# Storing the two float32r parts of each word of w_in side by side in an attention + MLP kernel

## The chip, the cores and the metric

The kernel runs on one core of a Trainium2 chip. The time is device microseconds of one execution of the whole program. Beside the bare times there is one execution with the hardware profiler on; all rows of a profile come from it.

## The reference

Two stages. Attention over 8 batches x 8 heads, with 1152 keys of 64 values per head and the queries averaged in neighbouring pairs, so 576 queries per head. Its output, 4608 tokens x 512, is the input x of a two-matrix MLP with 2048 hidden units. All inputs and the output are float32.

```python
q_pool = q.reshape(B, H, S // 2, 2, D).mean(axis=3)
scores = (1 / sqrt(D)) * q_pool @ k.T
attn = exp(scores - max(scores)); attn = attn / (sum(attn) + 1e-9)
x = (attn @ v) as [B * S // 2, H * D]          # 4608 x 512
h = x @ w_in                                   # w_in 512 x 2048
g = h - tanh(h)
out = g @ w_out                                # w_out 2048 x 512
```

## The kernel before

**Two parts for each number.** [...] The arriving w_in and w_out are int64 words on the host's side, that is, two 32-bit words for each weight, and the kernel makes the high and the low float32r part of each weight itself.

**Preparing the weights (class `W`, lines 411 to 475).** It runs during attention, in 16 blocks: four of w_in (one for each 128 rows, columns 0 to 1023), four of w_out, four of w_in (columns 1024 to 2047), four of w_out. A block is 128 partitions x 1024 weights. `load` fetches the block twice, once as it is (`w_raw`) and once shifted by two bytes (`w_off`); both are seen as int32 with two words for each weight, and the views `self.hw` and `self.mid` take every second word. `steps` lists six steps, which attention takes from a list at fixed places, four for each head pair from the third pair on: `begin` (ScalarE, absolute value of w_raw into w_t), `clamp` (three VectorE instructions on w_t), `mid` (VectorE, w_off into the low half of the tile `w_hl`), `high` (VectorE, w_raw and w_t into the high half of w_hl; then the next block's loads are issued), an unnamed one (VectorE, high half of w_hl into w_t), and `low` (VectorE, low half of w_hl in place; then `store`). The tile w_hl exists once, so a block's `mid` waits until the stores of the block before have read it. In w_hl the 1024 high parts lie ahead of the 1024 low ones.

**Where the weights rest.** `store` writes w_hl to a scratch tensor in HBM: `wi_dram`, indexed by block f of 128 hidden units, partition, part s (high or low), row block c and hidden unit n; and `wo_dram` for w_out. For w_in it issues two DMAs on SyncE's queue, one for each part, each with runs of 128 words. Later `load_w` (line 101) fetches 128 x 1024 words for each of the 16 values of f, 4 KB in each partition, into whatever tile is free (w_raw, w_off, w_hl, w_t, raw, q, and tiles of their own named w), and keeps a view of it indexed by s, c and n in `wi[f]`.

**Attention.** 32 head pairs, each with 18 places of scores and exponentials and 18 places of P times V. Scores are four pairs of 64-row matmuls for each place; row maxima of the next pair are taken by VectorE from PSUM (mx). All PSUM results of this stage go through a ring of four buffers (ps). Into the last three pairs the first three steps of the MLP are put.

**The MLP.** 9 chunks of 512 tokens x 16 blocks of 128 hidden units = 144 steps. For each step `hidden` (line 165) issues twelve matmuls into ps_h: the weights are `wi[f][:, w, c]`, 128 x 128, and the moving operand is 512 tokens of x's high or low part (the very last step is done in two halves of 256 tokens). `shrink` then computes g on ScalarE, VectorE and GpSimd, and `second` issues twelve matmuls for the output two steps later; there g is the weight operand (g_hi, g_lo) and w_out moves.

**Order.** The order of each engine's instructions is as they are written out: `InOrder` (line 27) chains every instruction to the one before it on its engine, SyncE's DMA issues among them. The line numbers of most rows are therefore L37, the helper's; rows are told apart by tiles.

Of the kernel before, what the change touches and what calls it, by code (L numbers as in the profile page):

```python
# [7 lines left out]
F32 = mybir.dt.float32  # L8
F32R = mybir.dt.float32r
I32 = mybir.dt.int32  # L10
# [36 lines left out]
def attention_ffn_kernel(  # L47
# [16 lines left out]
    P = 128  # L64
    B, NP, _, _, SQ = q.shape
# [7 lines left out]
    DM, DFF = w_in.shape  # L73
    w_in, w_out = w_in.bitcast(U16), w_out.bitcast(U16)
    NF = DFF // P
    n_pair = B * NP
    pe, act, dve, pool, sp = (InOrder(tc, e) for e in (nc.tensor, nc.scalar, nc.vector, nc.gpsimd, nc.sync))

    const = ctx.enter_context(tc.tile_pool(name="const", bufs=1))
    dram = ctx.enter_context(tc.tile_pool(name="scratch", bufs=1, space=DRAM))  # L80
# [5 lines left out]
    s_dram = dram.tile([B, NP, 2, SQ], F32, name="s_dram")  # L86
    r_dram = dram.tile([B, NP, 2, SQ], F32, name="r_dram")
    m_dram = dram.tile([2, 2, P * 4 * 32], F32, name="m_dram")
    wi_dram = dram.tile([NF, P, 2, NP, P], F32, name="wi_dram")
    wo_dram = dram.tile([NF, P, 2, DM], F32, name="wo_dram")  # L90

    xp = [ctx.enter_context(tc.tile_pool(name="xp0", bufs=1))]
# [2 lines left out]
    wp = ctx.enter_context(tc.tile_pool(name="wp", bufs=1))  # L95
# [3 lines left out]
    wi, wo = {}, {}  # L99

    def load_w(tile_, f, which):

        t = tile_[:, which * 1024:(which + 1) * 1024] if tile_.shape[1] == 2048 else tile_[:, 0:1024]
        sp.dma_start(t.bitcast(F32), (wi_dram, wo_dram)[which][f].rearrange("p s n -> p (s n)" if which else "p s c n -> p (s c n)"))
        if which == 0:
            wi[f] = t.rearrange("p (s c n) -> p s c n", s=2, c=NP)
        else:
            wo[f] = t.rearrange("p (s n) -> p s n", s=2)

# [104 lines left out]
    def store(c, j):  # L214
        o = outp[0].tile([P, DM], F32, name="o_f")
        act.activation(o, c.po[j], AF.Copy)
        sp.dma_start(out[c.t0 + j * P:c.t0 + (j + 1) * P], o)
# [11 lines left out]
    with ExitStack() as actx:  # L229
# [178 lines left out]
        WN = 1024  # L408
        lo_b, hi_b = 2.0 ** -15, float.fromhex("0x1.dffffep+16")

        class W:
# [17 lines left out]
            def steps(self, then):  # L429
                ts, stt = dve.tensor_scalar, dve.scalar_tensor_tensor  # L430

                def f(x):
                    return x.bitcast(F32)

                def begin():
                    self.t = wp.tile([P, WN], I32, name="w_t")
                    act.activation(f(self.t), f(self.raw)[:, :, 1], AF.Abs)

                def mid():
                    self.hl = wp.tile([P, 2, WN], I32, name="w_hl")  # L440
                    ts(self.hl[:, 1], self.mid, 0x01FFFFFF, None, op0=ALU.bitwise_and)

                def clamp():
                    ts(f(self.t), f(self.t), lo_b, hi_b, op0=ALU.max, op1=ALU.min)
                    ts(self.t, self.t, 0x08000000, 3, op0=ALU.bitwise_xor, op1=ALU.logical_shift_left)
                    ts(self.t, self.t, 0x7FFFFFFF, None, op0=ALU.bitwise_and)

                def high():
                    stt(self.hl[:, 0], self.hw, -0x80000000, self.t, op0=ALU.bitwise_and, op1=ALU.bitwise_or)
                    if then:  # L450
                        then.load()

                def low():
                    stt(self.hl[:, 1].bitcast(F32R), self.hl[:, 1], 2.0 ** -36, f(self.t), op0=ALU.mult, op1=ALU.mult)
                    self.store()

                return [
                    begin,
                    clamp,
                    mid,  # L460
                    high,
                    lambda: ts(self.t, self.hl[:, 0], -0x800000, None, op0=ALU.bitwise_and),
                    low,
                ]

            def store(self):
                for s in range(2):
                    src = self.hl[:, s].bitcast(F32)
                    if self.kind == 0:
                        f0 = self.c // P  # L470
                        sp.dma_start(wi_dram[f0:f0 + WN // P, :, s, self.i].rearrange("f p n -> p f n"),
                                     src.rearrange("p (f n) -> p f n", n=P))
                    else:
                        sp.dma_start(wo_dram[self.i:self.i + 2, :, s].rearrange("f p n -> p f n"),
                                     src.rearrange("p (f n) -> p f n", n=DM))

        blocks = [W(0, r, 0) for r in range(NP)] + [W(1, i, 0) for i in range(0, 8, 2)]
        blocks += [W(0, r, WN) for r in range(NP)] + [W(1, i, 0) for i in range(8, 16, 2)]
# [45 lines left out]
        def first_weights(f, name, which):  # L524
            t = (wp if name[0] == "w" else rawp if name == "raw" else qp).tile(
                [P, {"w_t": 1024, "raw": KQ, "q2": 2 * SQ}.get(name, 2048)], F32R, name=name)
            for i in which:
                load_w(t, f, i)
# [28 lines left out]
        for pi in range(n_pair):  # L557
# [7 lines left out]
            n = pi + EARLY - n_pair  # L565
            if n == 0:
                c = Chunk(0)
# [29 lines left out]
    for f in range(NF):  # L597
        for which, have in enumerate((wi, wo)):
            if f not in have:
                load_w(wt.tile([P, 1024], F32R, name=f"w{which}_{f}"), f, which)  # L600
        if f == 7:
            nxt.fetch()
            for c in range(2):
                nxt.fetch_r(c)

    xs = None
    for ci in range(len(chunks)):
        if ci:
            c = Chunk(ci)
# [4 lines left out]
        for f in range(NF):  # L614
            n = ci * NF + f
            s = steps[n]
# [15 lines left out]
            if f == 1 and ci:  # L632
                for j in range(4):
                    store(steps[n - 2].chunk, j)
# [13 lines left out]
    for i, k in enumerate(b.parts):  # L648
        g_high(b, k)
        g_low(b, k)  # L650
        for j in range(2 * i, 2 * i + 2):
            second(b, [j])
            store(b.chunk, j)
# [38 lines left out]
```

## Time and profile before

| | us |
|---|---|
| median of 3 runs | 1580.03 |
| lowest and highest | 1577.24, 1580.16 |
| the profiled execution | 1580.02 |
| its span, from first to last instruction | 1578.3 |
| busy in it: TensorE matmul / weight load | 1556.5 / 1224.1 |
| busy in it: VectorE / ScalarE / GpSimd | 1185.8 / 978.3 / 1155.3 |

The granted TensorE clock is 0.999 over the span. PE is TensorE's matmuls, PEld its weight loads, which overlap the matmuls; DVE is VectorE, ACT ScalarE, POOL GpSimd, SP SyncE. A row of a group reads: line, engine, operation, output tile <- input tiles, partitions x elements, xcount | busy us, mean ns of one | idle us of the engine before them, and what ended it. Matmuls overlap each other and their ends are modelled, so the spacing of their starts says more than their lengths.

### The profile page before, as it was taken

Reading aid. Unit: us, or ns where it says so; the run is one execution under the profiler, and the core shown is the slowest. Engines: PE = TensorE matmul, PEld = TensorE weight load, DVE = VectorE, ACT = ScalarE, POOL = GpSimd, SP = SyncE. Lnnn points to the kernel's source line nnn. Section 1 sums busy time; section 2 is a strip of 40 time slices with the busy share of each in tenths; the row PEclk is TensorE's granted clock in tenths of the full one; section 3 lists DMA queues with packets and bytes.
Section 4 is the critical chain, followed back from the end, with each engine's and each line's share of the span. In section 5 each row is a group of like instructions: output and inputs, shape, how many; then the busy total and the mean of one; then the engine's idle time right before and its main releaser. Section 6 shows DMA issues by size and latency. Waiting matters only on the chain.

```text
span 1578.3 us, 30802 instructions
## 1 busy us (share of the span) xinstructions
PE 1556.5 (99%) x12012; PEld 1224.1 (78%) x12012; DVE 1185.8 (75%) x1558; ACT 978.3 (62%) x1617; POOL 1155.3 (73%) x813
## 2 busy tenths in 40 slices
PE   7999999999999999999999999999999999999998
PEld 5777777777777777676778888888888888888886
DVE  6588787888888887765457777777777777777776
ACT  5667667667667667675645655565555555565654
POOL 6788888898888897785857576666767575766664
PEclk9999999999999999999999999999999999999999
DMA  5757767768677769573171201010010101020000
GB/s 169 207 177 218 222 185 220 218 211 252 186 237 210 218 201 267 143 231 91 63 285 70 68 15 67 14 61 14 13 61 14 67 14 67 14 67 14 28 1 27
DMA packets 88676, 193.59 MB, mean 123 GB/s; under 512 B 12882, under 2 KB 39890, under 8 KB 86482
## 3 DMA queue, kind: packets, MB, share of 16 engines
q1 hardware_dynamic: 79746, 155.35, 27.4%
q0 software_dynamic: 8784, 36.28, 12.7%
q8 instruction: 94, 1.54, 0.4%
q14 instruction: 52, 0.43, 0.1%
HBM read 126.12 MB, written 38.04 MB: 104 GB/s over the span
## 4 chain that ended last, share of the span: by engine, by line
PE 91%; DMA 3%; ACT 2%; DVE 2%; issue 1%; SPq 0%; POOLq 0%; POOL 0%; ACTq 0%; DVEq 0%
PE ps L37 43%; PE ps_o L37 24%; PE ps_h L37 24%; ACT p L37 2%; DMA s_dram<-s_s 2%; DVE mx L37 1%; DMA m_row<-m_dram 0%; DMA x_r<-r_dram 0%; DMA m_dram<-tr 0%; DVE w_hl L37 0%; SPq L37 0%; DVE w_t L37 0%; DMA q<-in_q_dram 0%; DVE ps_w L37 0%; DVE x_r L37 0%
## 5 line engine op out<-in xcount | busy, mean ns | idle before, releaser
L37 DVE TENSOR_REDUCE mx<-ps 128x2 f32<-128x768 f32 x448 | 400.1, 924 | 145.2 <-PE ps L37 145.0
L37 POOL TENSOR_SCALAR g_m<-g_u 128x512 uint8<-128x512 f32 (+1 forms) x145 | 247.2, 1705 | 184.6 <-ACT g_u L37 170.3
L37 POOL TENSOR_TENSOR sum<-p,p 128x576 f32<-128x576 f32 x192 | 294.4, 1533 | 117.9 <-ACT p L37 117.9
L37 ACT ACTIVATE p<-ps 128x576 f32<-128x576 f32 x576 | 347.3, 653 | 48.0 <-PE ps L37 27.6
L37 POOL TENSOR_TENSOR sum<-sum,p 128x576 f32<-128x576 f32 x192 | 291.7, 1519 | 15.0
L37 PE MATMUL ps<-p,v 128*64 128x288 f32 x2304 | 286.4, 407 | 3.5 <-DVE mx L37 0.4
L37 PE MATMUL ps<-kq_h 64*128 64x288 f32 (+1 forms) x1920 | 273.4, 338 | 8.4 <-ACT kq_h L37 6.4
L37 PEld LDWEIGHTS ps<-p,v 128*64 128x64 f32 x2304 | 162.5, 137 | 119.6 <-ACT p L37 10.2
L37 POOL TENSOR_TENSOR g_lo<-g_s,g_hi 128x512 fp32r<-128x512 f32 (+1 forms) x145 | 186.9, 1289 | 87.4 <-ACT g_hi L37 87.4
L37 PE MATMUL ps_o<-w,g_hi 128*128 128x512 f32 x792 | 244.0, 389 | 1.0 <-ACT g_hi L37 1.0
L37 ACT ACTIVATE g_u<-ps_h 128x512 f32<-128x512 f32 (+1 forms) x142 | 84.0, 591 | 217.8 <-PE ps_h L37 216.3
L37 PEld LDWEIGHTS ps<-kq_h 64*128 64x128 f32 x1920 | 179.1, 186 | 49.6 <-issue 13.9
L37 DVE SCALAR_TENSOR_TENSOR ps_w<-g_u,ps_h 128x512 f32<-128x512 f32 (+1 forms) x142 | 98.4, 693 | 153.2 <-ACT g_t L37 153.2
L37 PE MATMUL ps_h<-x_h,w 128*128 128x512 f32 (+1 forms) x800 | 212.0, 387 | 0.1
L37 ACT ACTIVATE g_s<-g_u,pc 128x512 f32<-128x512 f32 x290 | 193.4, 715 | 11.4 <-POOL g_lo L37 0.2
L37 PE MATMUL ps<-m_row,sel 64*128 64x288 f32 x1152 | 171.4, 293 | 2.8 <-DMA m_row<-m_dram 2.2
L37 PEld LDWEIGHTS ps_o<-w,g_hi 128*128 128x128 f32 x792 | 148.5, 188 | 32.1 <-ACT g_hi L37 1.4
L37 PEld LDWEIGHTS ps_h<-x_h,w 128*128 128x128 f32 x800 | 149.3, 188 | 31.1 <-DVE g_t L37 0.5
L37 PE MATMUL ps<-kq_l,kq_h 64*128 64x288 f32 x1152 | 171.7, 293 | 0.0
L37 PE MATMUL ps<-kq_h,kq_l 64*128 64x288 f32 x1152 | 171.6, 293 | 0.0
L37 PE MATMUL ps_o<-w,g_lo 128*128 128x512 f32 x396 | 154.4, 390 | 0.1
L37 DVE COPY_PREDICATED g_s<-g_m,g_t 128x512 f32<-128x512 uint8 (+1 forms) x145 | 110.5, 762 | 17.0 <-POOL g_m L37 2.1
(114 smaller groups left out, 2379.7 us busy)
## 6 DMA issues: line engine op xcount, KB each, us to landing
kq_l<-raw POOLq DMA_DIRECT2D x31, 864.0 KB, 8.0
v<-in_v_dram SPq DMA_DIRECT2D x32, 576.0 KB
raw<-in_k_dram SPq DMA_DIRECT2D x31, 576.0 KB
x_dram<-o_s SPq DMA_DIRECT2D x32, 288.0 KB
x_l<-x_dram SPq DMA_DIRECT2D x9, 1024.0 KB
out_dram<-o_f SPq DMA_DIRECT2D x36, 256.0 KB
raw<-in_q_dram SPq DMA_DIRECT2D x30, 288.0 KB
raw<-in_q_dram POOLq DMA_DIRECT2D x30, 288.0 KB, 10.0
```

What stands on the lines that cost most here:

```text
L37: i = f(*args, **kwargs)
```

## The change

The high and the low part of a w_in weight become neighbours: in w_hl while a w_in block is prepared (the three VectorE steps that write it step over every second word, and the step that reads the high half does too), in wi_dram, and in the loaded tiles. The view `wi[f]` keeps its indices, so `hidden` is unchanged in the text, but the 128 columns of each of its weight loads now lie two words apart. A w_in block is stored by one DMA with runs of 256 words instead of two with runs of 128. The w_out blocks, their stores and loads, and the output matmuls stay as they were.

```diff
-    wi_dram = dram.tile([NF, P, 2, NP, P], F32, name="wi_dram")
+    wi_dram = dram.tile([NF, P, NP, P, 2], F32, name="wi_dram")
...
-        sp.dma_start(t.bitcast(F32), (wi_dram, wo_dram)[which][f].rearrange("p s n -> p (s n)" if which else "p s c n -> p (s c n)"))
+        sp.dma_start(t.bitcast(F32), (wi_dram, wo_dram)[which][f].rearrange("p s n -> p (s n)" if which else "p c n s -> p (c n s)"))
         if which == 0:
-            wi[f] = t.rearrange("p (s c n) -> p s c n", s=2, c=NP)
+            wi[f] = t.rearrange("p (c n s) -> p s c n", s=2, c=NP)
...
                 def mid():
-                    self.hl = wp.tile([P, 2, WN], I32, name="w_hl")
+                    self.hl_t = wp.tile([P, 2 * WN], I32, name="w_hl")
+                    self.hl = self.hl_t.rearrange("p (s n) -> p s n" if self.kind else "p (n s) -> p s n", s=2)
                     ts(self.hl[:, 1], self.mid, 0x01FFFFFF, None, op0=ALU.bitwise_and)
...
             def store(self):
+                if self.kind == 0:
+                    f0 = self.c // P
+                    sp.dma_start(wi_dram[f0:f0 + WN // P, :, self.i].rearrange("f p n s -> p f (n s)"),
+                                 self.hl_t.bitcast(F32).rearrange("p (f n) -> p f n", n=2 * P))
+                    return
                 for s in range(2):
-                    src = self.hl[:, s].bitcast(F32)
-                    if self.kind == 0:
-                        f0 = self.c // P
-                        sp.dma_start(wi_dram[f0:f0 + WN // P, :, s, self.i].rearrange("f p n -> p f n"),
-                                     src.rearrange("p (f n) -> p f n", n=P))
-                    else:
-                        sp.dma_start(wo_dram[self.i:self.i + 2, :, s].rearrange("f p n -> p f n"),
-                                     src.rearrange("p (f n) -> p f n", n=DM))
+                    sp.dma_start(wo_dram[self.i:self.i + 2, :, s].rearrange("f p n -> p f n"),
+                                 self.hl[:, s].bitcast(F32).rearrange("p (f n) -> p f n", n=DM))
```

## The prediction

> **What bounds the kernel now.** I read the page's head first, then its chain of work that ended last, then that chain in order of time.
>
> ```profile
> span 1578.3 us, 30802 instructions
> PE 1556.5 (99%) x12012; PEld 1224.1 (78%) x12012; DVE 1185.8 (75%) x1558; ACT 978.3 (62%) x1617; POOL 1155.3 (73%) x813
> ...
> PE 91%; DMA 3%; ACT 2%; DVE 2%; issue 1%; SPq 0%; POOLq 0%; POOL 0%; ACTq 0%; DVEq 0%
> ```
>
> TensorE sets the end: it is 91% of the chain. The chain in order of time (start, length, what) shows two regimes.
>
> ```profile
> 105.52 22.52 PE ps L37 x253
> 129.37 22.52 PE ps L37 x253
> ...
> 583.00 12.01 PE ps L37 x107
> ...
> 656.69 22.52 PE ps L37 x253
> 680.54 11.31 PE ps L37 x99
> ...
> 796.20 3.04 PE ps_o L37 x12
> 799.23 2.72 PE ps_h L37 x12
> 801.95 2.72 PE ps_o L37 x12
> 804.67 2.72 PE ps_h L37 x12
> ```
>
> In attention one head pair takes 129.37 - 105.52 = 23.85 us. In the MLP, from 796.20 us to the end, every block of twelve matmuls takes 2.72 us, for h (ps_h) and for the output (ps_o) alike: 2.72 / 12 = 0.2267 us per matmul. The change touches the weights of the ps_h blocks and the stage in attention that prepares them, so I looked at both.
>
> **The weight loads, where the change could cost most.** First the timeline of TensorE matmuls (start, length of the merged stretch, operation), from a steady stretch and from the last step, where the moving width is halved to 256:
>
> ```profile
> 1201.63 1.07 PE L37 MATMUL ps_h<-x_h,w 128*128 128x512 f32 x4
> 1202.54 1.07 PE L37 MATMUL ps_h<-x_l,w 128*128 128x512 f32 x4
> 1203.44 1.07 PE L37 MATMUL ps_h<-x_h,w 128*128 128x512 f32 x4
> ...
> 1559.91 1.12 PE L37 MATMUL ps_h<-x_h,w 128*128 128x256 f32 x8
> 1560.88 0.64 PE L37 MATMUL ps_h<-x_l,w 128*128 128x256 f32 x4
> 1561.36 0.64 PE L37 MATMUL ps_h<-x_h,w 128*128 128x256 f32 x4
> ```
>
> Starts are (1203.44 - 1201.63) / 8 = 0.226 us apart at 512 columns, and (1561.36 - 1560.88) / 4 = 0.120 us apart at 256. Each of these matmuls has a weight load of its own, 128 columns of one block of w_in. Halving the moving width takes 0.107 us off the spacing, so at 512 the moving side sets it. At 256 loads follow one another every 120 ns, so a load with its words side by side occupies the load path for at most 120 ns. The groups of weight loads by shape (busy, mean ns of one) bound it from the other side:
>
> ```profile
> L37 PEld LDWEIGHTS ps_h<-x_h,w 128*128 128x128 f32 x800 | 149.3, 188 | 31.1 <-DVE g_t L37 0.5
> L37 PEld LDWEIGHTS ps<-p,v 128*64 128x64 f32 x2304 | 162.5, 137 | 119.6 <-ACT p L37 10.2 <-DVE tr L37 0.7 <-DVE mx L37 0.7
> L37 PEld LDWEIGHTS ps<-sum,ones 128*32 128x32 f32 x768 | 21.8, 109 | 23.1 <-issue 8.8
> ```
>
> From 64 to 128 columns a load grows by 188 - 137 = 51 ns, 0.80 ns a column; from 32 to 64 by 28 ns, 0.88. At 0.80, 128 columns stream in 102 ns, and the other 86 ns are a latency that overlaps the next load. So the occupancy today lies between 102 ns (my estimate) and 120 ns, and the next matmul asks for its weights every 226.7 ns. **The cover is 226.7 / 120 = 1.89 at the least and 226.7 / 102 = 2.2 by the estimate.** A strided load may cost that much more before TensorE notices.
>
> What does a stride of two words cost a reader? No weight load of before has one, but other engines read with it: `mid` and `high` read words 1, 3, 5... of w_off and w_raw, `begin` reads w_raw so on ScalarE. The instructions on w_hl (duration min/median/max), and ScalarE's groups:
>
> ```profile
> L37 DVE TENSOR_SCALAR w_hl<-w_off x16: 650/1270/1892, 88.5 to 634.9; 128x1024 int32<-128x1024 int32 x16
> L37 DVE SCALAR_TENSOR_TENSOR w_hl<-w_raw,w_t x16: 1209/1820/2434, 90.3 to 635.4; 128x1024 int32<-128x1024 int32 x16
> L37 DVE TENSOR_SCALAR w_t<-w_hl x16: 649/1219/1899, 108.2 to 639.6; 128x1024 int32<-128x1024 int32 x16
> L37 DVE SCALAR_TENSOR_TENSOR w_hl<-w_hl,w_t x16: 1226/2310/2316, 108.8 to 641.5; 128x1024 fp32r<-128x1024 int32 x16
> ```
>
> ```profile
> L37 ACT ACTIVATE kq_h<-raw 128x1728 fp32r<-128x1728 f32 x31 | 51.0, 1645 | 8.0 <-DMA raw<-in_q_dram 4.1 <-POOL raw L37 3.9
> L37 ACT ACTIVATE g_hi<-g_s 128x512 fp32r<-128x512 f32 x143 | 88.8, 621 | 1.3 <-DVE g_s L37 1.3
> L37 ACT ACTIVATE w_t<-w_raw 128x1024 f32<-128x1024 f32 x16 | 18.7, 1170 | 30.0 <-DVE w_hl L37 30.0
> ```
>
> On VectorE a strided source costs nothing: 650 ns for w_off against 649 ns for the contiguous w_hl, and 1209 against 1226 for the two-source form (minima, since the medians carry interference). On ScalarE contiguous rows give (1645 - 621) / (1728 - 512) = 0.842 ns a column, so 1024 columns would take 621 + 512 x 0.842 = 1052 ns; the strided read takes 1170, 11% more. With 11%, a weight load goes from 102 to 113 ns, or from 120 to 133. At 226.7 ns it is hidden either way. In the last step, 24 matmuls of 256 columns, it costs 24 x 13 ns = 0.3 us at worst.
>
> The bounds: below, nothing, since a load that is already hidden can't gain by becoming longer, and I know no row in which a strided read is faster. Above, I take a halved rate, each fetch bringing one useful word instead of two: 2 x 102 = 204 ns is hidden still, while 2 x 120 = 240 ns is 13.3 ns too long. The loops give 9 chunks x 16 blocks = 144 steps of 12 matmuls; 143 steps, 1716 matmuls, are full width. That makes 1716 x 13.3 ns = 22.9 us, and the 24 half-width ones lose another 24 x 120 ns = 2.9 us: 25.8 us together. I take **0**, since the measured strided reads lie between 0% and 11% and the cover is 89% or more; 0 to 25.8 us goes into the range.
>
> [...]
>
> **The VectorE writes in attention.** In the eight w_in blocks `mid`, `high` and `low` now write every second word, and the step after `high` and `low` read so (free, as above). No row of before shows a strided write. Bounds: nothing, as for reads, or a halved rate, which adds the time of 1024 more columns; the two-source form streams its 1024 in 1209 ns, so 1.1 us an instruction: 3 x 1.1 = 3.3 us a block, 26 us of VectorE time in all. It is covered by VectorE's idle time, as the stages show (window, its length, PE, PEld, DVE, ACT, POOL busy, granted clock, DMA share, GB/s): two pairs with w_in work, two without any.
>
> ```profile
> 116.85:164.56 47.71, 47.51 (x536) 35.64 (x538) 40.66 (x46) 32.38 (x51) 40.07 (x28) 1.00 0.73 196
> 668.02:715.71 47.69, 47.50 (x536) 35.62 (x538) 28.95 (x38) 31.84 (x51) 38.06 (x28) 1.00 0.74 216
> ```
>
> VectorE does 11.7 us more in the first, and the two pairs take 47.71 against 47.69 us: TensorE doesn't see it. A block spans 1.5 pairs, so its idle time is 7.05 x 0.75 = 5.3 us, more than 3.3. The same instruction already swings by 1.2 us between 650 and 1892 ns while the pairs stay at 23.85. If the cover were gone, the row maxima (mx) behind these instructions would free their PSUM slots late, and the next scores matmuls would wait. I take 0, with 0 to 5 us for the range (a fifth of the 26).
>
> **The stores.** Two stores of 512 KB for each w_in block become one of 1 MB, with runs of 1 KB instead of 512 B.
>
> ```profile
> L37 SPq DMA_DIRECT2D wi_dram<-w_hl x16: 366/432/912, 110.9 to 497.4; - x16
> ...
> L37 SPq DMA_DIRECT2D w<-wi_dram x11: 319/423/606, 796.8 to 823.8; - x11
> ```
>
> SP issues eight fewer, 8 x 0.432 = 3.5 us of its queue. Nobody on the chain waits for it: from 105.52 to 583.00, all of the w_in stores included, twenty pairs take 477.48 us, 23.874 each, or 0.5 us in all above 23.85. So fewer packets gain 0.5 us at most, and I count 0. The next block's `mid` must now wait for the whole store instead of its half. The rows of w_hl in the window 108 to 140 us show the room:
>
> ```profile
> L37 DVE SCALAR_TENSOR_TENSOR w_hl<-w_hl,w_t x2: 2304/2306/2309, 108.8 to 136.9; 128x1024 fp32r<-128x1024 int32 x2
> L37 DVE TENSOR_SCALAR w_hl<-w_off x1: 651/651/651, 132.0 to 132.0; 128x1024 int32<-128x1024 int32 x1
> ```
>
> One block's `low` starts at 108.8 and ends 2.3 us later, the next block's `mid` starts at 132.0, 20.9 us after that; 1 MB at the 196 GB/s of the window above takes 5.3 us. The reloads stay 4 KB per partition, and none is added.
>
> **Sum.** 0 (loads) + 0 (writes) + 0 (stores). The profiled execution took 1580.02 us, its span plus 1.7 us around it, and the median of the three runs is 1580.03. **Forecast: 1580.0 us**, own range 1577 to 1583, as the three runs already spread from 1577.24 to 1580.16.
>
> **Rivals.** (1) *The load becomes the bound of the ps_h blocks.* The place is each of the 1740 w_in matmuls, and it decides as soon as a strided load occupies more than 226.7 ns. For it: the contiguous load may occupy all of the 120 ns, so doubling would pass the point. Against it: the 0 to 11% of the other engines' strided reads. At 240 ns the time is 1580.0 + 25.8 = 1606; an occupancy between 226.7 and 240 gives less, down to 1580.0 + 24 x 0.107 = 1583, and a longer one more, 1.7 us for each nanosecond. [...] (2) *Strided writes hold up the row maxima.* It decides when a block adds more than its 5.3 us of idle VectorE time, or piles up in one place so that all four PSUM slots are held. At a fifth of 26 us the time is 1585. Against it: the two window rows. (3) *The smaller packet count speeds attention up.* The 0.5 us above cap it: 1579.5, not to be told from no change. For more, the steady 0.2267 us would have to fall, and nothing here shortens the moving side. (4) *The change doesn't do what it says*: the strided operand is split into more than one load for each matmul. Two loads of 64 columns at their 137 ns take 274 ns if they do not overlap, 47 ns over the spacing: 1716 x 47 = 81 us, 1661 us. The page's count of weight loads would show it.
>
> **How the numbers follow.** About 0.2%, 3.2 us, is what a measurement of this kernel can tell from no change. No change, rival 3 in it: 0.65. Rival 1: 0.22, of which I put two thirds at or below 240 ns, 1606 us. Rival 2: 0.05. Rival 4: 0.03. Faster by over 0.2%, by something that I don't see: 0.05. So faster 0.05, same 0.65, slower 0.30. The range goes from 1576 to 1607: it holds the 0.65, rival 2, two thirds of rival 1 and a little of the faster side, some 0.85. The likeliest case by itself has 1577 to 1583.
>
> **What would show it.** The ps_h blocks in the chain keep 2.72 us (right) or grow above the ps_o blocks of 2.72 us (rival 1: 2.88 at 240 ns). The weight loads of ps_h may show more than 188 ns without harm up to some 290 (188 + 102). In the last step the spacing stays near 0.120 us, or shows the occupancy of a strided load directly: the most telling row. The strided VectorE forms stay near 650 and 1209 ns at the least, and pairs stay at 23.85 us. The count of weight loads stays 12012. The forecast is wrong if ps_h blocks and ps_o blocks no longer take the same time.

## The result, and the profile after

The changed kernel takes 1591.37 us (median of four runs, 1589.08 to 1595.39) against 1578.81 us for the kernel before (four runs, 1577.24 to 1580.16). The ratio is 1.0084, with a 95% interval of 1.0062 to 1.0106: 12.6 us slower. The forecast was 1580.0.

The profiled execution took 1589.08 us. Its chain of work in order of time (start, length, what), at the start and the end of the MLP:

```profile
793.14 3.02 PE ps_o L37 x12
796.17 2.80 PE ps_h L37 x12
798.97 2.73 PE ps_o L37 x12
801.69 2.80 PE ps_h L37 x12
...
1564.37 2.81 PE ps_h L37 x12
```

The h blocks, which took 2.72 us before, take 2.80; the output blocks stay at 2.73. From the first ps_h block after attention to the last are 139 steps: (1564.37 - 796.17) / 139 = 5.527 us a step. In the chain of before the same stretch begins at 799.23, a row that the prediction shows, and ends at

```profile
1555.39 2.73 PE ps_h L37 x12
```

which gives 756.16 / 139 = 5.440. The difference, 0.087 us a step, is 12.1 us over the 139 steps. The whole MLP, from the first output block to the end of the span, grew from 1578.3 - 796.2 = 782.1 us to 1587.3 - 793.1 = 794.2.

Attention ended 3.1 us earlier in this execution. That is not the change's doing, as far as the profiles show: in the profiled execution of before, one chain of transfers held up TensorE once, late in attention.

```profile
692.31 13.49 DMA s_dram<-s_s
...
707.26 4.39 DMA m_dram<-tr
...
711.67 6.70 DMA m_row<-m_dram
...
718.40 12.48 PE ps L37 x145
```

In the profiled execution of the changed kernel TensorE's stretches follow one another at 23.85 us there:

```profile
681.32 22.52 PE ps L37 x253
705.17 22.52 PE ps L37 x253
```

The hold-up comes and goes between executions of either layout: of the experiments below with the layout of before it is in the profile of e1 and not in that of e3, and of those with the changed layout in that of e12 and not in that of e2. So the span grew by 9.0 us, the medians by 12.6, and the MLP alone by 12.1.

The weight loads by shape, after:

```profile
L37 PEld LDWEIGHTS ps_h<-x_h,w 128*128 128x128 f32 x800 | 153.6, 193 | 31.4 <-DVE g_t L37 0.4
L37 PEld LDWEIGHTS ps_o<-w,g_hi 128*128 128x128 f32 x792 | 148.6, 188 | 32.8 <-ACT g_hi L37 1.4
```

A strided load is shown as 193 ns instead of 188. And the timeline of TensorE in the last step, whose moving width is 256:

```profile
1568.90 1.12 PE L37 MATMUL ps_h<-x_h,w 128*128 128x256 f32 x8
1569.86 0.64 PE L37 MATMUL ps_h<-x_l,w 128*128 128x256 f32 x4
1570.34 0.64 PE L37 MATMUL ps_h<-x_h,w 128*128 128x256 f32 x4
```

(1570.34 - 1569.86) / 4 = 0.120 us, as before. So with a load that is hardly longer, and that fits into 120 ns, matmuls that followed one another every 227 ns now do so every 233. This is what the experiments are about.

The preparation and the stores did what was expected. The instructions on w_hl (duration min/median/max) and SP's stores:

```profile
L37 DVE TENSOR_SCALAR w_hl<-w_off x16: 650/1272/1894, 89.3 to 635.6; 128x1024 int32<-128x1024 int32 x16
L37 DVE SCALAR_TENSOR_TENSOR w_hl<-w_raw,w_t x16: 1211/1820/2467, 91.1 to 636.2; 128x1024 int32<-128x1024 int32 x16
L37 DVE TENSOR_SCALAR w_t<-w_hl x16: 650/1214/1901, 109.0 to 640.4; 128x1024 int32<-128x1024 int32 x16
L37 DVE SCALAR_TENSOR_TENSOR w_hl<-w_hl,w_t x16: 1224/2315/2318, 109.7 to 642.3; 128x1024 fp32r<-128x1024 int32 x16
...
L37 SPq DMA_DIRECT2D wi_dram<-w_hl x8: 366/378/382, 112.0 to 498.2; - x8
```

All four forms stand where they stood, within 5 ns at the median. Half of these sixteen are w_out blocks, which the change leaves alone. In the w_in blocks by themselves, `mid` takes 654 ns where nothing holds it up (650 to 653 before), `high` 1212 to 1215 (1209 to 1214), the step that reads the high half 651 to 653 (651 to 652) and `low` 2310 to 2317 (2304 to 2316). Where `high` is held up, by about 1.2 us in both kernels, it grew by up to 35 ns. One such `mid`, in the window 108 to 140 us, for which the prediction shows 651 ns:

```profile
L37 DVE TENSOR_SCALAR w_hl<-w_off x1: 654/654/654, 132.8 to 132.8; 128x1024 int32<-128x1024 int32 x1
```

### The profile page after: what moved, and what is told of

Same layout as the page of the kernel before. It is cut to its first block, busy times and chain, and to the rows that moved or that the text cites. A ratio compares the mean times of both kernels' runs of the same rounds, so it can differ in the third digit from the quotient of the medians.

```text
span 1587.3 us, 30798 instructions
## 1 busy us (share of the span) xinstructions
PE 1567.7 (99%) x12012; PEld 1232.5 (78%) x12012; DVE 1185.2 (75%) x1558; ACT 977.4 (62%) x1617; POOL 1149.6 (72%) x813
## 3 DMA queue, kind: packets, MB, share of 16 engines
q0 software_dynamic: 8784, 36.28, 12.6%
## 4 chain that ended last, share of the span: by engine, by line
PE 93%; ACT 2%; DVE 2%; DMA 1%; issue 1%; SPq 0%; POOLq 0%; POOL 0%; ACTq 0%; DVEq 0%
PE ps L37 44%; PE ps_h L37 25%; PE ps_o L37 24%; ACT p L37 2%; DVE mx L37 1%; DMA s_dram<-s_s 1%; DMA x_r<-r_dram 0%; DVE w_hl L37 0%; DVE w_t L37 0%; DMA q<-in_q_dram 0%; DVE ps_w L37 0%; DVE x_r L37 0%; SPq L37 0%; ACT g_s L37 0%; DVE g_s L37 0%
## 5 line engine op out<-in xcount | busy, mean ns | idle before, releaser
L37 POOL TENSOR_SCALAR g_m<-g_u 128x512 uint8<-128x512 f32 (+1 forms) x145 | 242.7, 1674 | 192.0 <-ACT g_u L37 177.0
L37 PE MATMUL ps_h<-x_h,w 128*128 128x512 f32 (+1 forms) x800 | 217.0, 392 | 0.0
L37 PEld LDWEIGHTS ps_h<-x_h,w 128*128 128x128 f32 x800 | 153.6, 193 | 31.4 <-DVE g_t L37 0.4
```

Source lines behind the costliest of these rows:

```text
L37: i = f(*args, **kwargs)
```

## The experiments

Spacing means the distance between the starts of two matmuls of one group, averaged over the steady part of the MLP (the first of each group left out). It is worked out from the trace's starts in nanoseconds.

**One part at a time.** e1 is the kernel before with the strided view alone; e2 is the changed kernel with the contiguous view.

```diff
 # e1, on the kernel before; e2 is the reverse, on the changed kernel
-            wi[f] = t.rearrange("p (s c n) -> p s c n", s=2, c=NP)
+            wi[f] = t.rearrange("p (c n s) -> p s c n", s=2, c=NP)
```

> The kernel before, with one line changed: the view of a loaded w_in tile takes its 128 weight columns two words apart. Preparation, stores and reloads stay as before, so the h matmuls multiply with other words of the same tile; the work is the same in kind and count. Theory R (reading with a stride costs, wherever the data came from): the spacing in the h blocks is 233.3 ns as in the changed kernel, blocks of 2.80 us, the output blocks 2.72 to 2.73, and the time some 12 us over before (143 steps x 86 ns = 12.3). Rival P (the layout in memory, the stores or the order of preparing costs): spacing 226.7 ns, blocks 2.72 us, the time of before.

> The changed kernel with the one line undone that makes the weight loads strided: stored and loaded side by side, read by TensorE with neighbouring words (so it multiplies with other words of the tile). Theory R: blocks of 2.72 us and the time of before, within 0.2%; the merged stores and strided VectorE writes show nothing, pairs stay at 23.85 us. Rival P: blocks of 2.80 us, 12 us over before.

e1: 1589.19 us against 1577.47, ratio 1.0081 (1.0055 to 1.0107). e2: 1578.26, ratio 1.0000 (0.9985 to 1.0014). The chains, first e1, then e2:

```profile
908.59 2.80 PE ps_h L37 x12
911.39 2.73 PE ps_o L37 x12
```

```profile
906.92 2.72 PE ps_h L37 x12
909.64 2.72 PE ps_o L37 x12
```

Spacing 233.3 and 226.7 ns. The loss comes from TensorE reading its weights with a stride, and none that e2 can tell, to some 2 us, from layout, stores or VectorE's writes: theory R.

**Wider strides.** Views four and eight words apart, on the kernel before.

```diff
-            wi[f] = t.rearrange("p (s c n) -> p s c n", s=2, c=NP)
+            wi[f] = t.rearrange("p (s n c) -> p s c n", s=2, c=NP)    # e3: four words
+            wi[f] = t.rearrange("p (n s c) -> p s c n", s=2, c=NP)    # e4: eight words
```

> The kernel before with weight columns four words apart in the view (other words of the tile are multiplied). [...]

> The kernel before with weight columns eight words apart in the view (other words of the tile are multiplied). [...]

e3: 1595.86 us, ratio 1.0112 (1.0097 to 1.0127). e4: 1617.12, ratio 1.0253 (1.0234 to 1.0271). The loads, e3 first, then e4:

```profile
L37 PEld LDWEIGHTS ps_h<-x_h,w 128*128 128x128 f32 x800 | 202.2, 310 | 4.2 <-DVE g_t L37 0.4
```

```profile
L37 PEld LDWEIGHTS ps_h<-x_h,w 128*128 128x128 f32 x800 | 211.9, 330 | 4.0 <-DVE g_t L37 0.2
```

Here the load has become the bound: at 256 moving columns the spacing is 233.2 ns in e3 and 241.6 in e4, where it was 120. The last step of e3:

```profile
1576.64 1.10 PE L37 MATMUL ps_h<-x_l,w 128*128 128x256 f32 x4
1577.57 1.10 PE L37 MATMUL ps_h<-x_h,w 128*128 128x256 f32 x4
```

Four spacings are 0.93 us. At 512 columns the spacing is 234.9 and 245.1 ns. So the price is not the same for every stride above one word: at 512 columns it is 6.6 ns at two words, 8.2 at four and 18.4 at eight. At four words the 256-column spacing is 1.94 times that of before, about half the rate, and between four and eight words there is a further 8 to 10 ns. The loads are shown as 193 ns at two words, 310 at four and 330 at eight; why the large step lies between two and four words, no run shows.

**The load's own time, and what the moving width does to it.** Five chunks with their moving operands cut, side by side (e6), two words apart (e7) and four words apart (e9).

```diff
+        cuts = {3: (384,), 4: (256,), 5: (128, 256, 384), 6: (448,), 7: (192,)}.get(s.chunk.t0 // 512, ())
+        parts = [slice(a, b) for a, b in zip((0,) + cuts, cuts + (512,))] if cuts else s.parts
-        for k in s.parts:
+        for k in parts:
```

> The kernel before, with the moving operand of the h matmuls cut into pieces in five of the nine chunks: 384 + 128 columns in chunk 3, 256 + 256 in chunk 4, four times 128 in chunk 5, 448 + 64 in chunk 6, 192 + 320 in chunk 7. Each piece loads its weights again, so the kernel does more loads and is slower as a whole; only the spacing of the matmuls within each group counts. [...]

> The changed kernel (two words apart) with the same cuts. Measured so far: 233.3 ns at 512 against 226.7, and 120 at 256 as before. [...] Theory O (the load itself is longer than 120 ns when words are two apart, and the 256-column group of the last step is no steady state): over 120 ns at 64 to 256.

> The kernel before with the view four words apart (it multiplies with other words of the tile) and the same cuts. Measured so far: 233.3 ns at 256 columns and about 235 at 512. [...] If it depends on the moving side, it grows from 64 to 512.

A finer set followed, with cuts at 480, 496, 464, 416 and 504 (e10 side by side, e11 two words apart).

> The kernel before with the h matmuls of five chunks cut into wide and narrow pieces: 480 + 32 columns in chunk 3, 496 + 16 in chunk 4, 464 + 48 in chunk 5, 416 + 96 in chunk 6, 504 + 8 in chunk 7. The narrow pieces load their weights too, so only the spacing within each group counts. [...]

> The changed kernel (words two apart) with the same cuts. Known against side by side: 120 and 120 ns at 256, 173.6 and 173.3 at 384 once steady, 203.4 and 202.3 at 448, 233.3 and 226.7 at 512. [...] Theory I (loads and moving stream interfere, by an amount that depends on how the two periods fit): tolls between 0 and 7 ns that change from width to width without an order. Theory E (it grows towards 512): 416 under 2, 464 some 4, 480 some 5, 496 and 504 near 6 ns.

TensorE's timelines at 64 columns, for e6, e7 and e9:

```profile
1362.30 0.61 PE L37 MATMUL ps_h<-x_l,w_raw 128*128 128x64 f32 x4
1362.74 0.61 PE L37 MATMUL ps_h<-x_h,w_raw 128*128 128x64 f32 x4
```

```profile
1371.35 0.64 PE L37 MATMUL ps_h<-x_l,w_raw 128*128 128x64 f32 x4
1371.82 0.64 PE L37 MATMUL ps_h<-x_h,w_raw 128*128 128x64 f32 x4
```

```profile
1581.59 1.10 PE L37 MATMUL ps_h<-x_l,w_raw 128*128 128x64 f32 x4
1582.52 1.10 PE L37 MATMUL ps_h<-x_h,w_raw 128*128 128x64 f32 x4
```

Four spacings are 0.44, 0.47 and 0.93 us. Each of these runs is one execution; with their additional loads they take 1658.46 (e6), 1671.32 (e7), 1675.12 (e10), 1684.72 (e11) and 1966.89 us (e9), and only the spacings are compared. In e9 the granted clock fell as well, from 1.00 to 0.66 between these two windows (window, its length, PE, PEld, DVE, ACT, POOL busy, granted clock, DMA share, GB/s):

```profile
1200.00:1300.00 100.00, 100.00 (x438) 94.35 (x437) 50.21 (x74) 38.56 (x66) 39.07 (x30) 1.00 0.10 32
1380.00:1500.00 120.00, 120.00 (x467) 113.24 (x468) 29.86 (x44) 24.59 (x42) 24.60 (x18) 0.66 0.01 3
```

In the second window the h matmuls keep 233 to 234 ns while the output matmuls lie 426 ns apart at the median, so the column for four words can be read all the same; why the clock fell, no run shows. Mean spacing in ns, by moving width (8 to 48, 96, 416 and 464 to 504 from e10 and e11):

| width | side by side | two words | difference | four words |
|---|---|---|---|---|
| 8 to 48 | 111.7 | 117.8 | +6.1 | |
| 64 | 111.3 | 117.4 | +6.1 | 233.4 |
| 96 | 111.7 | 119.1 | +7.4 | |
| 128 | 111.7 | 117.9 | +6.2 | 233.7 |
| 192 | 112.0 | 118.2 | +6.2 | 234.5 |
| 256 | 120.0 | 119.7 | -0.3 | 233.3 |
| 320 | 146.9 | 146.7 | -0.2 | 233.3 |
| 384 | 176.2 | 173.4 | -2.8 | 234.3 |
| 416 | 186.7 | 187.1 | +0.4 | |
| 448 | 202.7 | 203.3 | +0.6 | 235.9 |
| 464 | 210.0 | 211.3 | +1.3 | |
| 480 | 216.6 | 220.0 | +3.4 | |
| 496 | 220.0 | 225.5 | +5.5 | |
| 504 | 227.3 | 226.7 | -0.6 | |
| 512 | 226.7 | 233.3 | +6.6 | 234.9 |

The narrow widths show the load by itself: 111.7 ns side by side, less than the 120 of the last step, 118 two words apart, 233 four words apart. From 256 to 448 the 118 ns are hidden, as the prediction had it. From 464 on something returns, up to the whole 6.6 ns, with 504 as an exception. Theory O falls: from 64 to 256 columns the spacing at two words is 117.4 to 119.7 ns, under 120. The toll does not come whole as soon as the moving side is the longer one (-0.2 ns at 320, +0.6 at 448), and it does not belong to 512 columns alone (+3.4 at 480, +5.5 at 496); theory E, a growth towards 512, falls at 504 (-0.6). What is left is I, a toll without an order, which I read as an interference of load and moving stream. The side-by-side column speaks for it too. A moving column takes (226.7 - 120.0) / 256 = 0.417 ns, and at 256, 320, 416, 496 and 512 the spacing is 13.3 ns over that; at 384, 448, 464, 480 and 504 it is another 3 to 4 ns above. At 384 the first matmuls of a group are 175 to 185 ns apart and the last ones 173: as if the two streams needed several matmuls to fall into step.

**The other half of the MLP.** Here w_in stays side by side, and the weights of the output matmuls are taken every second token.

```diff
-            ts = slice(j * P, (j + 1) * P)
             for i, (g, w) in enumerate(((s.g_h, 0), (s.g_h, 1), (s.g_l, 0))):
-                pe.matmul(po[j], g[:, ts], wo[s.f][:, w], ...)
+                g = g.rearrange("p (a n s) -> p a s n", a=2, s=2)[:, j // 2, j % 2]
+                pe.matmul(po[j], g, wo[s.f][:, w], ...)
```

> The kernel before, with the stride put on the other half of the MLP: the weights of the output matmuls (128 tokens of g) are taken every second token, and the rows of out are stored accordingly; the output is computed in full. w_in stays side by side. If the toll belongs to any weight load with words two apart: output blocks of 2.80 us, h blocks of 2.72, and about 12 us over before (144 steps x 86 ns = 12.4), a ratio of 1.008. If it is peculiar to the w_in tiles or to where they lie: output blocks of 2.72 us and the time of before.

1589.07 us against 1579.22, ratio 1.0056 (1.0036 to 1.0075). The chain:

```profile
904.50 2.80 PE ps_o L37 x12
907.30 2.73 PE ps_h L37 x12
```

The toll moves to the output blocks, with a spacing of 233.6 ns there and 226.7 in the h blocks. It does not belong to w_in's tiles. The ratio is a little under the 1.008 expected; the runs of before that it is compared with lay between 1576.55 and 1583.14.

**Addresses instead of strides.** If it is interference, the places of the operands in memory should matter without any stride. Rows of x's tiles 16 bytes further apart (e12 with the stride, e13 without), weight blocks 116 instead of 128 words apart with x as it was (e15) and with x shifted in step (e14), and rows of x 64 bytes further apart (e16 without the stride, e17 with it).

```diff
-            self.h = xp[ci % 2].tile([P, NP, 512], F32R, name="x_h")
+            self.h = xp[ci % 2].tile([P, NP, 516], F32R, name="x_h")[:, :, 0:512]   # x_l the same; 528 in e16, e17
...
-                pe.matmul(s.h[:, k], wi[s.f][:, w, c], x[:, c, k], ...)
+                pe.matmul(s.h[:, k], wi[s.f][:, 512 * w + 116 * c:512 * w + 116 * c + 128], x[:, c, k], ...)   # e14, e15
```

> The changed kernel with 4 unused words (16 bytes) after each 512 words of x's tiles, so the four moving operands of a step start at 0, 16, 32 and 48 bytes into a 64-byte piece and no longer all at the same place. If the toll hangs on where the two reads meet in memory (the low address bits of the moving operand against those of the weights), the spacing in the h blocks changes from 233.3 ns for some or all of the four. If it is the timing alone, 233.3 stays.

> The kernel before with the same 4 unused words after each 512 words of x's tiles. By the address theory the spacing of 226.7 ns may change for some of the four as well, by timing alone it stays 226.7.

> The kernel before with x's rows 16 bytes further apart and the four weight columns blocks of a step taken 116 words apart instead of 128 (overlapping, so it multiplies with other words of the tile). Both operands then start at 0, 16, 32 and 48 bytes of a 64-byte piece, in step with each other. If only the place of one against the other matters, 226.7 ns returns in the h blocks; if the moving operand's own place against that of the matmul before matters, it stays near 231.

> The kernel before with the weight blocks alone taken 116 words apart (other words of the tile; x as before): weights start at 0, 16, 32 and 48 bytes of a 64-byte piece, the moving operands all at 0. If the place of one against the other matters: 230 ns and more, as with x alone shifted (231.5). If only the moving operand's place matters: 226.7.

> The kernel before with x's rows 64 bytes further apart, so all four moving operands start at the same place of a 64-byte piece again, but not of a 256-byte piece. If the interference repeats every 64 bytes: 226.7 ns and blocks of 2.72 us; if it looks at a longer stretch of addresses: above 226.7, as at 16 bytes (231.5).

> The changed kernel with x's rows 64 bytes further apart. If the interference repeats every 64 bytes: 233.3 ns as in the changed kernel; if not, a spacing that changes from place to place, between 228 and 237 ns as at 16 bytes.

| kernel | weights | shifted | spacing of h, ns | one execution, us | before beside it |
|---|---|---|---|---|---|
| before | side by side | nothing | 226.7 | 1580.02 | |
| e13 | side by side | x, 16 bytes | 231.6 | 1592.27 | 1577.12 |
| e16 | side by side | x, 64 bytes | 233.4 | 1589.56 | 1583.23 |
| e15 | side by side | weights | 232.0 | 1592.59 | 1583.23 |
| e14 | side by side | both in step | 231.5 | 1594.57 | 1583.23 |
| after | two words | nothing | 233.3 | 1589.08 | |
| e12 | two words | x, 16 bytes | 232.6 | 1592.88 | 1577.12 |
| e17 | two words | x, 64 bytes | 231.0 | 1591.76 | 1583.23 |

The last two columns are single executions, so a few microseconds between them say nothing; the spacings carry the reading. TensorE's timeline in e15, where nothing but the start of the weight columns differs from before:

```profile
1204.29 1.09 PE L37 MATMUL ps_h<-x_h,w 128*128 128x512 f32 x4
1205.22 1.09 PE L37 MATMUL ps_h<-x_l,w 128*128 128x512 f32 x4
1206.14 1.09 PE L37 MATMUL ps_h<-x_h,w 128*128 128x512 f32 x4
```

(1206.14 - 1204.29) / 8 = 0.231 us. Its loads are shown as long as those of the kernel before, 188 ns, and at 256 columns its spacing is 118 ns:

```profile
L37 PEld LDWEIGHTS ps_h<-x_h,w 128*128 128x128 f32 x800 | 149.2, 188 | 33.7 <-DVE g_t L37 0.4
```

Every shift costs about as much as the stride, and with x shifted the stride itself adds +1.0 (e12 against e13) or -2.4 ns (e17 against e16). That the timing alone decides is out by this. It is not enough that the two operands keep their places against each other (e14), nor that they start at the same place of a 64-byte piece (e16). In the kernels with x shifted, later tiles lie elsewhere too, so these do not show which address decides; e15 moves no tile, and there the start of the weight columns alone is enough. In the changed kernel the blocks start elsewhere too, 1024 bytes apart and the low part 4 bytes on. But the stride is enough without that: in e8 the first two matmuls of an output block take their weights from the same start as in the kernel before, and lie 233.3 ns apart instead of 226.7.

## Why the prediction was wrong

**What bounds the kernel** was right: TensorE sets the end, attention pairs stay at 23.85 us, and the loss lies in the h blocks.

**The weight load's own cost** was right within its range. I expected 0% to 11% from the strided reads of VectorE and ScalarE; the narrow widths give 111.7 to 118 ns, 6%. The occupancy of 102 to 120 ns held as well. That a stride of two words does not halve the rate is shown, with 118 ns; four words, with 233, do.

**The step that failed** is "A strided load may cost that much more before TensorE notices", with the cover of 1.89. It took the load and the moving stream for two lines that only meet at the hand-over, so that a load shorter than 226.7 ns could cost nothing. The runs show that a load can cost time while it is hidden by a wide margin: 118 ns of load in a period of 227 ns cost 6.6 ns a matmul at 512 columns, and nothing at 256 to 384 (119.7 against 120.0 ns, and 173.4 against 176.2). Shifting the weights by some bytes costs 5.3 ns (e15), with loads that are shown no longer than before, 188 ns. What I had taken for the moving side's own time, 226.7 ns, holds only while the operands lie as they do in the kernel before; disturbed, it is 231 to 233. The stride ends that state, which would explain why it costs as much as a shift and little or nothing on top of one. That the two reads disturb each other in the memory is my guess, and it would account for all of this; no run shows the mechanism itself, nor the rule by which addresses matter, and both stay open.

**Rival 1** had the place and the sign, but not the mechanism. It was to decide at an occupancy over 226.7 ns, and the price of 13.3 ns a matmul belonged to that. Measured are 6.6 ns without the occupancy: of the 87 ns a step, 11 x 6.6 = 73 lie between the matmuls of an h block, and the other 14 in the three spacings where h and output blocks meet, which grew to 230 to 232.5 ns. The wide range, up to 1607 us, was stretched for this rival's sake; that it holds 1591.37 us is luck, since the time came by another way. A load that is the bound does exist at four words, in e3: 233 ns, and 1595.86 us. The row that I called the most telling, the last step's spacing, could not tell: at 256 columns both layouts take 120 ns.

**Rival 2** is out: e2 has the merged stores and the strided VectorE writes, and a ratio of 1.0000. Its interval, -0.15% to +0.14% or some 2 us either way, excludes the 5 us of rival 2. It can't tell the 0.5 us of **rival 3** from nothing, but the forecast counted that as no change. In the w_in blocks `mid` and `high` keep 654 and 1212 ns against 650 and 1209, so a step of two words costs the writes of these two 4 ns an instruction at most, and the read of the high half 1 ns (651 to 653 against 651 to 652). Rival 4 is out as well, with 12012 weight loads before and after.

**The 0 for the stores** holds, with 378 ns at the median for each of the eight issues.

## What to carry to other kernels

A weight load hidden behind its matmul was not free of charge here, where 118 ns of load in a period of 227 cost 6.6: ask not only whether it is shorter than the matmul, but also which words it reads, and from where. A steady spacing of matmuls can hang on how rows and blocks of the tiles are placed (226.7 ns before, 231.6 with a pad of 16 bytes in e13), so a change of layout, a pad of 16 bytes included, is to be judged by the spacing of the starts in the trace. Read TensorE's weights side by side where the layout is free to choose; two words apart cost 0.8% here, four 1.1%, eight 2.5%.

## What the runs showed of the hardware

A load of 128 float32r columns occupied the load path for 111.7 ns side by side (e6, e10), 118 at two words (e7, e11), 233 at four (e9) and about 242 at eight (e4, at 256 moving columns, where the load is the bound). A matmul of 512 columns with a fresh load followed the last after 226.7 ns when the moving rows lay 2048 bytes apart and the weight blocks 512 (before, e2), and after 231 to 233 ns with the weights two words apart and in every other placement tried (e12 to e17). After the h blocks' shifted reads the output blocks took up to nine matmuls of 225 to 236 ns to come back to 227 (e13). Their own rows and blocks are spaced as before there, but later tiles lie elsewhere because of the pads, so it stays open whether the h blocks' reads or the place does this.
